# Full-height operands and dummy products in the early stage of an mLSTM and two-layer expert kernel

## The chip, the core and the metric

The kernel runs on one core of a Trainium2 chip. The metric is the device time of one execution in microseconds (us); lower is better. TensorE (PE in the rows) does matrix products, VectorE (DVE), ScalarE (ACT) and GpSimd (POOL) do elementwise work, and SyncE (SP) issues most DMA transfers.

## What is computed

Three stages follow one another: an mLSTM attention over 4 batches, 8 heads, 768 tokens and 40 dimensions; a dense layer pair with a squared ReLU; and a routed layer pair with 8 experts, one for each token. The part that the change touches is the first:

```python
for t in range(S):
    kt, vt, qt = (k[:, :, t], v[:, :, t], q[:, :, t])
    m_new = np.maximum(f_gate[:, :, t] + m, i_gate[:, :, t])
    f_stab = np.exp(f_gate[:, :, t] + m - m_new)
    i_stab = np.exp(i_gate[:, :, t] - m_new)
    m = m_new
    C = f_stab[:, :, None, None] * C + i_stab[:, :, None, None] * np.einsum('bhd,bhe->bhde', vt, kt)
    n = f_stab[:, :, None] * n + i_stab[:, :, None] * kt
    h_tilde = np.einsum('bhde,bhe->bhd', C, qt)
    nq = np.einsum('bhd,bhd->bh', n, qt)[:, :, None]
    denom = np.maximum(np.abs(nq), 1.0)
    o = 1.0 / (1.0 + np.exp(-o_gate[:, :, t]))
    y[:, :, t] = o * h_tilde / denom
# dense: relu(x @ w_in)**2 @ w_out;  routed: the same shape with the expert of the largest logit
```

## The kernel before

The recurrence is worked in 24 chunks of 128 tokens (four batches, six chunks each). Chunks 0 to 2 are the first chunks of three batches; they need no carried state. For each chunk the kernel makes, head by head, the scores of keys against queries (`scores`, tile sp, L776), multiplies them by a decay matrix (`weigh`, DVE, L781), multiplies by the values (`values`, tile pv, L789), makes the state update (`update`, tile tp, L716), divides, gates, turns the result by three transposes (`across`, tile xpt, L725), and splits it into a high and a low half for the dense layer (`columns_out`). Three chunks make one group of 384 tokens; the first layer product of a group (`l1`, tile hp, L867) can start when its three chunks are split.

The decay matrix of chunks 0 to 2 is made on TensorE by `decays_early` (tile Ap): two mask products (L659, bf16, 128 rows), then for each of two tiles four products that spread a head's decays over the columns (L663) and one that adds the bias (L665). Their operands are the running decays A, the bias c, and columns of an identity; A and c have one row for each of 36 gate rows, so these products have 36 rows. The scores of chunks 0 to 6 take keys and queries as they were loaded, in float32 with 40 rows, one for each dimension; from chunk 7 on (`WHOLE`) they take 120 rows of split operands. Odd ones among the first seven chunks load keys and queries into a tile kqs, even ones into two tiles st. `gate_stage` makes A and c on DVE and POOL from the gates; `columns` in it turns three of its rows into columns by narrow transposes (tile pt, L470).

Beside this the dense weights are decoded in 16 blocks: loaded on SP (L525), rescaled, masked and joined on ACT, POOL and DVE (L536, L544, L558, L567), rounded to a high half w_h on ACT (L570), and the rest written as a low half w_l by POOL or DVE (L583).

The order of all this up to the first layer group is written out by hand in a string, `PLAN`. Each word issues one step: `de1` the decays of chunk 1, `sc1` its scores, `va1` and `vb1` its two halves of values, `up1` its update, `tu1` its three transposes, `L3` the low half of weight block 3, `l0` the first layer product. A word `f15` issues 15 dummy products: a 128x128 tile of ones times 512 columns of ones, in bf16, into a PSUM tile that nothing reads (L1400). Ahead of the plan stand `APART` one-column products of the same kind (L1420). Each engine works its own instructions in the order in which the words issued them, and waits where an input or a buffer isn't ready.

Of the kernel before, what the change touches and what calls it, by code (L numbers as in the profile page):

```python
# [9 lines left out]
F32 = mybir.dt.float32  # L10
# [15 lines left out]
L = 128  # L26
# [27 lines left out]
XC_DVE = 2  # L54
FETCH = 2
PERIOD = 6
APART = 54

AT_ONCE = 3
WHOLE = 7  # L60
KVO = 3
QK0, QK1, ROUND0, ROUND1 = 1, 3, (3, 4), (1, 2)
PLAN = """
    g0 A0 R0 g1 qk0 kv0 g2 g3 g4 g5 g6 f15 de0 ea0 A1 g7 A2 sc0 eb0 TP0 g8 R1 vw0 g9 de1 kv1 g10 g11 S0 th0 W0 H0 R2 A3 g12 TP1 ea1 wa0 va0 L0 wb0 vb0
    S1 TP2 W1 S2 up0 qk1 eb1 qk2 di0 W2 de2 A4 R3 T3 um0 ga0 A5 sc1 H1 du0 tu0 ea2 H2 kv2 vw1 L1 eb2 g13 S3 wa1 up1 va1 L2 wb1 um1 ou0 vb1 R4 th1 sc2
    W3 TP4 di1 R5 SA4 TP5 th2 wa2 wb2 de3 qk3 ga1 f3 va2 H3 A6 vw2 up2 vb2 ca3 W4 dup1 di2 f2 tu1 cb3 de4 ga2 dup2 g14 um2 ou1 f4 tu2 sc3 ea3 ou2 S5
    H4 L3 eb3 l0 R6 L4 l1 W5 A7 wa3 kv3 l2 ca4 T6 A8 in3 wb3 H5 sa0 l3 sa1 S6 sb0 m0 va3 W6 cb4 sa2 R7 l4 sbP1 L5 T7 qk4 sb2 m1 H6 vw3 sd3 vb3 S7 sa3
    R8 sb3 T8 W7 dt A9 l5 S8 up3 sa4 H7 m2 L6 l6 di3 th3 kv4 R9 m3 sc4 sa5 um3 sbP4 L7 W8 ccP3 ea4 A10 ga3 T9 de5 dup3 m4 sa6 H8 A11 sb5 S9 wa4 vw4
    LV8 R10 ca5 th4 T10 qk5 in4 W9 up4 eb4 tu3 A12 kv5 m5 sd4 wb4 R11 l7 ea5 S10 ou3 H9 cb5 sbP6 va4 W10 um4 vb4 T11 l8 m6 eb5 sc5 sa7 A13 sb7 sa8 di4
    L9 l9 S11 W11 R12 ccP4 sbP8 qk6 T12 H10 wa5 wb5 ga4 S12 sa9 th5 vw5 H11 m7 in5 R13 T13 va5 de6 up5 A14 vb5 L10 m8 W12 sd5 sbP9 l10 LV11 m9 du4  # L70
    SA13 H12 R14 di5 l11 sc6 A15 cb6 ca6 um5 sa10 L12 sbP10 T14 tu4 l12 sa11 R15 W13 S14 H13 m10 eb6 ccP5 sb11 L13 W14 m11 ea6 wb6 kv6 H14 T15 in6 wa6
    ga5 ou4 l13 qk7 L14 sa12 th6 va6 dup5 tu5 S15 l14 sbP12 sa13 W15 sd6 sb13 vb6 de7 vw6 ra7 ou5 m12 up6 H15 m13 LV15 sa14 ca7 cb7 di6 l15 rb7 sb14
    l16 ga6 sa15 l17 m14 kv7 du6 sa16 ea7 z tu6 sb15 sb16 eb7 um6 sa17 sb17 cc6 ou6 m15
""".split()


# [298 lines left out]
def kernel(ctx, tc, qk, q3, kvo, gates, w_io, wg, w12, cst, out, dbg=None):  # L375
# [68 lines left out]
    def gate_stage():  # L444

        R = S - L
        early, late = slice(0, L), slice(L, S)
        fi = scr[0:HR, 0:2 * S]
        nc.sync.dma_start(out=fi[:, 0:2 * L], in_=gates[:, 0:2 * L])
        f, i = (fi[:, 0:L], fi[:, 2 * L:2 * L + R]), (fi[:, L:2 * L], fi[:, 2 * L + R:])  # L450

        neg, one = [scr[:, 2 * S + 64 * k:2 * S + 64 * k + 64].bitcast(BF16) for k in range(2)]
        m, a, A, c, msk = flat[0:HR, 0:S + 1], *[flat[0:HR, S * k + 1:S * k + S + 1] for k in range(1, 5)]
        wv, eA = msk, a
        yield
        nc.vector.memset(m[:, 0:1], -1e30)
        nc.gpsimd.memset(msk, 1.0)
        nc.gpsimd.memset(msk.rearrange("p (c l) -> p c l", l=L)[:, :, 0:1], 0.0)
        nc.gpsimd.memset(neg, 0.0)
        nc.gpsimd.affine_select(out=neg, in_=neg, pattern=[[1, L]], compare_op=ALU.is_ge, fill=-1e30, base=0, channel_multiplier=-1)  # L460
        nc.gpsimd.tensor_copy(out=one, in_=ident)
        early_rows.extend((neg, one, A, c))
        yield
        nc.sync.dma_start(out=fi[:, 2 * L:], in_=gates[:, 2 * L:])
        yield

        def columns(src, dst, c0, c1):
            pt = psa.tile([128, 512], F32, tag="a", name="pt")
            for ch in range(c0, c1):
                nc.tensor.transpose(out=pt[:, HR * ch:HR * ch + HR], in_=src[:, L * ch:L * ch + L], identity=ident[0:HR, 0:HR])  # L470
            nc.scalar.activation(out=dst[:, c0:c1], in_=pt[:, HR * c0:HR * c1].rearrange("p (c h) -> p c h", h=HR), func=ACTF.Copy)

        for k, (part, c0, c1) in enumerate(((early, 0, 1), (late, 1, NCH))):
            lo, hi = part.start, part.stop
            n = c1 - c0
            chunked = lambda x: x[:, part].rearrange("p (c l) -> p c l", l=L)
            nc.vector.tensor_tensor_scan(out=m[:, lo + 1:hi + 1], data0=f[k], data1=i[k], initial=m[:, lo:lo + 1] if k else -1e30, op0=ALU.add, op1=ALU.max)
            yield
            nc.vector.tensor_tensor(out=a[:, part], in0=f[k], in1=m[:, lo:hi], op=ALU.add)
            nc.gpsimd.tensor_tensor(out=c[:, part], in0=i[k], in1=m[:, lo + 1:hi + 1], op=ALU.subtract)  # L480
            yield
            nc.vector.tensor_tensor(out=a[:, part], in0=a[:, part], in1=m[:, lo + 1:hi + 1], op=ALU.subtract)
            if k == 0:
                nc.vector.memset(a[:, 0:1], 0.0)
            yield
            nc.vector.tensor_tensor_scan(out=A[:, part], data0=msk[:, part], data1=a[:, part], initial=0.0, op0=ALU.mult, op1=ALU.add)
            nc.sync.dma_start(out=A_d[:, part], in_=A[:, part])
            yield
            nc.vector.tensor_tensor(out=c[:, part], in0=c[:, part], in1=A[:, part], op=ALU.subtract)
            if k:  # L490
                columns(c, cT, 0, NCH)
            yield
            nc.vector.tensor_tensor(out=chunked(wv), in0=chunked(c), in1=chunked(A)[:, :, L - 1:L].to_broadcast([HR, n, L]), op=ALU.add)
            nc.scalar.activation(out=wv[:, part], in_=wv[:, part], func=ACTF.Exp)
            columns(wv, wT, c0, c1)
            yield
        nc.scalar.activation(out=eA[:, late], in_=A[:, late], func=ACTF.Exp)
        columns(eA, eAT, 1, NCH)
        eAL = const.tile([HR, NCH], F32, name="eAL")
        nc.vector.memset(eAL[:, 0:1], 0.0)  # L500
        nc.vector.tensor_copy(out=eAL[:, 1:NCH].rearrange("p (c o) -> p c o", o=1), in_=chunked(eA)[:, :, L - 1:L])
        nc.gpsimd.dma_start(out=L_d, in_=eAL)
        w_l.append(wts.tile([128, NF - NE, IO], F32R, tag="late", name="w_l2"))
        yield
# [98 lines left out]
    where = [divmod(n, 3) for n in range(NC)]  # L603
    first = [sum(GROUPS[:g]) for g in range(len(GROUPS) + 1)]
    xT = {}

    class Chunk:

# [13 lines left out]

        def qk(self):

            self.st = []
            odd = at1.tile([120, 2, H * L], F32, tag="kq", name="kqs") if self.n < WHOLE and self.n % 2 else None
            for j in range(2):
                st = at2.tile([120, H * L], F32, tag="st", name="st") if odd is None else odd[:, j]
                rows = D if self.n < WHOLE else 3 * D
                nc.sync.dma_start(out=st[0:rows], in_=qk[self.b, self.c, j, 0:rows])  # L630
                self.st.append(st)
            if self.c > 0:
                self.q3 = at2.tile([120, 3, L], F32, tag="q3", name="q3")
                nc.sync.dma_start(out=self.q3.rearrange("p g l -> p (g l)"), in_=q3[self.b, self.c])
# [19 lines left out]
        def decays_early(self):  # L654
            neg, one, A, c = early_rows
            self.Ab, self.Ap = [None] * 2, []
            for j in range(2):
                self.Ap.append(psa.tile([128, 4, L], F32, tag="a", name="Ap"))
                nc.tensor.matmul(self.Ap[j], one, neg.rearrange("p (o l) -> p o l", o=1).to_broadcast([128, 4, L]), start=True, stop=False)  # L659
            for j in range(2):  # L660
                for h in range(4):
                    r = HB * self.b + 2 * h + j
                    nc.tensor.matmul(self.Ap[j][:, h], ident[0:HR, r:r + 1].to_broadcast([HR, L]), A[:, 0:L], start=False, stop=False)  # L663
                r = HB * self.b + j
                nc.tensor.matmul(self.Ap[j], c[:, 0:L], ident[0:HR, r:r + 7:2].rearrange("p (h o) -> p h o", o=1).to_broadcast([HR, 4, L]), start=False, stop=True)  # L665

        def causal(self, j):
            if self.n < AT_ONCE:
# [68 lines left out]
    class Main:  # L737
# [816 lines left out]
```

## Time and profile before

| | |
|---|---|
| median of 3 runs | 796.86 us (795.98 to 800.27) |
| profiled execution, its own time | 799.19 us |
| its span, first to last instruction | 797.4 us |
| granted TensorE clock, mean over the span | 0.955 of full |
| TensorE busy | 769.4 us, 96% |
| VectorE busy | 503.2 us, 63% |
| ScalarE busy | 407.7 us, 51% |
| GpSimd busy | 388.8 us, 49% |

Read the clock beside the busy time: a busy engine at half clock passes half the columns. The ends of matmuls are modelled, so the distance from one group's start to the next tells more than the length of a row. The view of stretches gives, for each, its length, the busy time and count of each engine, and then the granted clock, the share of DMA engines and GB/s. The chain of waits is the work that ended last, followed back; each of its rows has a start, a length and the work. A timeline row has start, length, engine, line, operation, output and inputs, shapes, count, and in brackets the idle time ahead and what ended it.

### The profile page before, as it was taken

The page shows a single profiled execution, that of the slowest core. Times are in us where ns is not written, and L with a number is a line of the kernel's source. Part 1 is how long each engine was busy: PE and PEld are TensorE (multiplying, and loading weights), DVE is VectorE, ACT ScalarE, POOL GpSimd, SP SyncE. Part 2 cuts the span into 40 slices and gives each one's busy share as a digit, 9 for nine tenths or more (in the row PEclk, how much of TensorE's full clock was granted, in tenths as well). Part 3 has the DMA queues.
Part 4 walks back from the last instruction along what each step waited for, and adds up shares of the span by engine and source line. Part 5 has one row for each costly group of instructions (what it writes and reads, how often), then busy time and mean ns, then how long its engine had stood idle before and what let it go on. Part 6 is the DMA issues. An engine that isn't in the chain of part 4 may idle for free.

```text
span 797.4 us, 14304 instructions
## 1 busy us (share of the span) xinstructions
PE 769.4 (96%) x5198; PEld 744.6 (93%) x5198; DVE 503.2 (63%) x1102; ACT 407.7 (51%) x760; POOL 388.8 (49%) x430
## 2 busy tenths in 40 slices
PE   9999998989899999999999999999989999999995
PEld 6789988989899999999999999999989999999995
DVE  6448998587576676666568655362547455867553
ACT  3337776445644644644544443554246555866453
POOL 6338999455655553563445300422136444556630
PEclk8558999999999999999999999999989999999998
DMA  7367865454754445344445000100168655875620
GB/s 259 90 166 207 242 172 145 118 146 114 216 164 143 115 115 142 105 112 143 113 113 171 1 1 31 32 31 1 60 224 272 187 174 169 250 236 189 223 60 15
DMA packets 55045, 109.01 MB, mean 137 GB/s; under 512 B 6896, under 2 KB 34681, under 8 KB 54834
## 3 DMA queue, kind: packets, MB, share of 16 engines
q1 hardware_dynamic: 50370, 95.88, 40.8%
q0 software_dynamic: 4160, 11.77, 4.5%
q8 instruction: 47, 0.77, 0.4%
q10 hardware_dynamic: 432, 0.29, 0.1%
q14 instruction: 36, 0.29, 0.1%
HBM read 98.69 MB, written 10.86 MB: 137 GB/s over the span
## 4 chain that ended last, share of the span: by engine, by line
PE 73%; POOL 10%; DVE 6%; DMA 5%; issue 3%; ACT 2%; SPq 0%; POOLq 0%; DVEq 0%; ACTq 0%
PE hp L867 17%; PE hp L289 12%; PE acc L900 5%; PE acc L901 5%; PE acc L902 5%; PE pv L789 4%; DMA st<-in_qk_dram 4%; PE op L309 4%; PE op L308 4%; PE op L310 4%; POOL kq L644 3%; PE sp L776 3%; PE tp L716 2%; POOL Ab L672 2%; PE lp L965 1%
## 5 line engine op out<-in xcount | busy, mean ns | idle before, releaser
L644 POOL TENSOR_TENSOR kq<-st,kq 120x256 fp32r<-120x256 f32 x136 | 101.3, 778 | 72.8 <-ACT kq L641 72.8
L900 PE MATMUL acc<-w_h,gh 128*128 128x320 f32 x384 | 124.5, 324 | 0.0
L867 PE MATMUL hp<-xh,w_h 128*128 128x384 f32 x384 | 114.7, 353 | 5.9 <-DVE gl L887 4.2
L902 PE MATMUL acc<-w_h,gl 128*128 128x320 f32 x384 | 118.8, 310 | 1.4 <-POOL gl L887 1.4
L901 PE MATMUL acc<-w_l,gh 128*128 128x320 f32 x384 | 118.4, 308 | 0.0
L875 ACT ACTIVATE g<-hp 128x384 f32<-128x384 f32 x128 | 62.1, 485 | 89.7 <-PE hp L867 88.9
L884 DVE SCALAR_TENSOR_TENSOR hp<-hp,g 128x384 f32<-128x384 f32 x121 | 67.5, 558 | 51.1 <-ACT g L875 51.0
L258 DVE SCALAR_TENSOR_TENSOR gl<-hp,gh 128x384 fp32r<-128x384 f32 x88 | 47.0, 553 | 70.1 <-ACT gh L228 65.6
L867 PE MATMUL hp<-xh,w_l 128*128 128x384 f32 x384 | 88.7, 339 | 0.1
L867 PE MATMUL hp<-xl,w_h 128*128 128x384 f32 x256 | 87.6, 342 | 0.0
L887 DVE TENSOR_TENSOR gl<-hp,gh 128x384 fp32r<-128x384 f32 x121 | 67.5, 558 | 12.6
L902 PEld LDWEIGHTS acc<-w_h,gl 128*128 128x128 f32 x384 | 72.2, 188 | 1.7 <-POOL gl L887 1.7
L867 PEld LDWEIGHTS hp<-xh,w_h 128*128 128x128 f32 x384 | 66.2, 191 | 7.8 <-DVE gl L887 5.0
L900 PEld LDWEIGHTS acc<-w_h,gh 128*128 128x128 f32 x384 | 72.6, 189 | 0.1
L901 PEld LDWEIGHTS acc<-w_l,gh 128*128 128x128 f32 x384 | 72.6, 189 | 0.0
L876 ACT ACTIVATE gh<-g 128x384 fp32r<-128x384 f32 x128 | 67.2, 525 | 6.3 <-PE acc L901 2.3
L867 PEld LDWEIGHTS hp<-xh,w_l 128*128 128x128 f32 x384 | 69.7, 190 | 0.7 <-POOL w_l L583 0.7
L228 ACT ACTIVATE gh<-hp 128x384 fp32r<-128x384 f32 x88 | 42.7, 491 | 43.4 <-PE hp L289 36.8
L685 POOL TENSOR_TENSOR vw<-kvo,wT 128x378 f32<-128x378 f32 x20 | 18.5, 925 | 88.3 <-DMA kvo<-in_kvo_dram 46.1
L641 ACT ACTIVATE kq<-st,cs 120x1024 fp32r<-120x1024 f32 x34 | 38.9, 1145 | 41.6 <-DMA st<-in_qk_dram 38.4
L679 ACT ACTIVATE Ab<-Ab 128x512 f32<-128x512 f32 x42 | 26.2, 628 | 61.2 <-POOL Ab L673 61.0
L789 PEld LDWEIGHTS pv<-kvo,Ab 128*128 128x128 f32 x384 | 53.2, 209 | 0.6 <-issue 0.3
(277 smaller groups left out, 1925.6 us busy)
## 6 DMA issues: line engine op xcount, KB each, us to landing
st<-in_qk_dram SPq DMA_DIRECT2D x34, 480.0 KB
raw<-in_w_dram SPq DMA_DIRECT2D x30, 512.0 KB
kvo<-in_kvo_dram SPq DMA_DIRECT2D x24, 529.0 KB
raw<-in_w_io_dram SPq DMA_DIRECT2D x16, 704.0 KB
Ab<-A_d SPq DMA_DIRECT2D x42, 256.0 KB
raw<-in_w_dram SPq DMA_DIRECT2D x20, 427.0 KB
raw<-in_w_dram SPq DMA_DIRECT2D x10, 426.0 KB
q<-in_q_dram SPq DMA_DIRECT2D x20, 180.0 KB
```

The source lines that it names most:

```text
L258: e.scalar_tensor_tensor(out=gl[:, j], in0=hp[j % 4], scalar=0.0, in1=gh[:, j].bitcast(F32), op0=ALU.max, op1=ALU.subtract).then_inc(sGL, 1)
L289: m = e.matmul(hp[f % 4][:, 0:w], a, c, start=(n == 0), stop=(n == 7))
L644: nc.gpsimd.tensor_tensor(out=o[:, c], in0=self.st[j][:, c], in1=o[:, c].bitcast(F32), op=ALU.subtract)
L789: nc.tensor.matmul(self.pv[:, hd], d.Ab[r][:, i], d.v[:, hd], start=True, stop=True)
L867: nc.tensor.matmul(hp, a, x, start=(n == 0), stop=(n == 7))
L875: nc.scalar.activation(out=r, in_=hp, func=ACTF.Relu)
L876: nc.scalar.activation(out=gh, in_=r, func=ACTF.Square)
L884: e.scalar_tensor_tensor(out=sq, in0=hp, scalar=0.0, in1=r, op0=ALU.max, op1=ALU.mult)
L887: e.tensor_tensor(out=gl, in0=sq, in1=gh.bitcast(F32), op=ALU.subtract)
L900: nc.tensor.matmul(acc[t][:, 0:DM], gh[:, sl], wh, start=(f == 0), stop=False)
L901: nc.tensor.matmul(acc[t][:, 0:DM], gh[:, sl], wl, start=False, stop=False)
L902: nc.tensor.matmul(acc[t][:, 0:DM], gl[:, sl], wh, start=False, stop=end)
```

## The change

It has three parts. The products of `decays_early` take all 128 rows of A, c and the identity, and the scores of chunks 0 to 6 take 120 rows of keys and queries; the rows that held nothing are set to zero once, by memsets on DVE, in tiles that live through the early chunks. A word `f2`, two dummy products, stands in `PLAN` ahead of nearly each early product group, 22 times, in place of `f3`, `f2` and `f4`. `APART` goes from 54 to 19.

```diff
-APART = 54
+APART = 19
-    S1 TP2 W1 S2 up0 qk1 eb1 qk2 di0 W2 de2 A4 R3 T3 um0 ga0 A5 sc1 H1 du0 tu0 ea2 H2 kv2 vw1 L1 eb2 g13 S3 wa1 up1 va1 L2 wb1 um1 ou0 vb1 R4 th1 sc2
+    L0 wb0 f2 vb0 S1 TP2 W1 S2 f2 up0 qk1 eb1 qk2 di0 W2 f2 de2 A4 R3 T3 um0 ga0 A5 f2 sc1 H1 du0 f2 tu0 ea2 H2 kv2 vw1 L1 eb2 f2 g13 S3 wa1 f2 up1 f2 va1
...
+        A0, cc0 = [flat[:, S * k + 1:S * k + 1 + L] for k in (2, 3)]
         yield
+        for x in padded[0]:
+            nc.vector.memset(x, 0.0)
+        nc.vector.memset(A0, 0.0)
+        nc.vector.memset(cc0, 0.0)
...
-        early_rows.extend((neg, one, A, c))
+        early_rows.extend((neg, one, A0, cc0))
...
+            if k == 0:
+                nc.vector.memset(kqs, 0.0)
             columns(wv, wT, c0, c1)
...
+    kqs = at1.tile([120, 2, H * L], F32, tag="kq", name="kqs")
+    padded = [[at2.tile([120, H * L], F32, tag="st", name="st") for _ in range(2)], [kqs[:, 0], kqs[:, 1]]]
...
+            self.st = padded[self.n % 2] if self.n < WHOLE else [at2.tile([120, H * L], F32, tag="st", name="st") for _ in range(2)]
+            rows = D if self.n < WHOLE else 3 * D
             for j in range(2):
+                nc.sync.dma_start(out=self.st[j][0:rows], in_=qk[self.b, self.c, j, 0:rows])
...
-                    nc.tensor.matmul(self.Ap[j][:, h], ident[0:HR, r:r + 1].to_broadcast([HR, L]), A[:, 0:L], start=False, stop=False)
+                    nc.tensor.matmul(self.Ap[j][:, h], ident[:, r:r + 1].to_broadcast([128, L]), A, start=False, stop=False)
-                nc.tensor.matmul(self.Ap[j], c[:, 0:L], ident[0:HR, r:r + 7:2].rearrange("p (h o) -> p h o", o=1).to_broadcast([HR, 4, L]), start=False, stop=True)
+                nc.tensor.matmul(self.Ap[j], c, ident[:, r:r + 7:2].rearrange("p (h o) -> p h o", o=1).to_broadcast([128, 4, L]), start=False, stop=True)
...
-                k, q = (d.st[j][0:D, c] for j in range(2)) if n < WHOLE else (d.kq[:, j, c] for j in range(2))
+                k, q = (d.st[j][:, c] for j in range(2)) if n < WHOLE else (d.kq[:, j, c] for j in range(2))
```

TensorE, from the narrow transposes of c (pt) through the values of chunk 0 (pv) and its update (tp) to the masks of the third decays (Ap), before:

```order
L470 MATMUL pt<-cs,flat 128x36 x6
L789 MATMUL pv<-kvo,Ab 128x42 x8
L716 MATMUL tp<-vw,kvo 120x126 x3
L659 LDWEIGHTS scr
L659 MATMUL Ap<-scr 128x512
```

The same place in the changed kernel, where the lines of the file have moved by six:

```order
L475 MATMUL pt<-cs,flat 128x36 x6
L1406 LDWEIGHTS ones
L1406 MATMUL warm<-ones 128x512
L1406 LDWEIGHTS ones
L1406 MATMUL warm<-ones 128x512
L795 MATMUL pv<-kvo,Ab 128x42 x4
L1406 LDWEIGHTS ones
L1406 MATMUL warm<-ones 128x512
L1406 LDWEIGHTS ones
L1406 MATMUL warm<-ones 128x512
L795 MATMUL pv<-kvo,Ab 128x42 x4
```

A pair of dummies now stands between the transposes and the values and between the two halves of values; the order of the other work is the same.

DVE, from the start of the program to the first operation on the late gates (640 columns), before:

```order
L456 MEMSET flat 36x1
L477 SCALAR_TENSOR_TENSOR flat<-scr 36x128
L479 TENSOR_TENSOR flat<-scr,flat 36x128
L482 TENSOR_TENSOR flat<-flat 36x128
L484 MEMSET flat 36x1
L486 SCALAR_TENSOR_TENSOR flat<-flat 36x128
L489 TENSOR_TENSOR flat<-flat 36x128
L493 TENSOR_TENSOR flat<-flat 36x128
L477 SCALAR_TENSOR_TENSOR flat<-scr,flat 36x640
```

And the first rows of the changed kernel, in two pieces:

```order
L458 MEMSET st 120x1024 x2
L459 MEMSET flat 128x128
L460 MEMSET flat 128x128
L461 MEMSET flat 36x1
L482 SCALAR_TENSOR_TENSOR flat<-scr 36x128
```

```order
L498 TENSOR_TENSOR flat<-flat 36x128
L501 MEMSET kqs 120x2048
L482 SCALAR_TENSOR_TENSOR flat<-scr,flat 36x640
```

The memsets of st and of the rows of A and c stand ahead of the first scan, that of kqs behind the early gate work and ahead of the late scan. On SP the loads into st now wait for their memset.

## Rows read from the trace of the kernel before

**Rows 1.** Stretches: busy time and count by engine, granted clock, DMA.

```profile
core 0: us, PE busy (x) PEld busy (x) DVE busy (x) ACT busy (x) POOL busy (x), PEclk, DMA share, GB/s
5.00:10.00 5.00, 5.00 (x24) 2.58 (x23) 2.49 (x4) 0.84 (x1) 1.32 (x2) 1.00 0.96 262
10.00:15.00 5.00, 5.00 (x30) 3.72 (x28) 4.90 (x5) 2.63 (x6) 2.86 (x2) 0.78 0.88 357
15.00:20.00 5.00, 5.00 (x17) 3.64 (x17) 3.76 (x5) 1.53 (x2) 4.75 (x4) 0.50 0.66 207
65.00:70.00 5.00, 5.00 (x26) 5.00 (x25) 4.49 (x7) 2.98 (x6) 3.51 (x4) 0.76 0.71 209
70.00:75.00 5.00, 5.00 (x37) 5.00 (x36) 4.00 (x6) 4.94 (x9) 4.92 (x5) 1.00 0.63 67
170.00:180.00 10.00, 7.54 (x45) 7.10 (x45) 7.12 (x29) 3.45 (x9) 1.04 (x2) 0.83 0.85 243
```

**Rows 2.** The chain of waits, 0 to 150 us: start, length, work.

```profile
1.01 1.61 PE apart L1420 x54
2.66 5.00 PE warm L1400 x15
7.66 0.43 PE Ap L659 x2
...
11.79 0.03 PE pt L470
...
55.42 0.85 PE warm L1400 x2
56.28 0.64 PE xpt L725 x3
56.92 0.68 PE pt L470 x5
...
63.77 6.05 PE hp L867 x24
...
73.19 0.82 PE pv L789 x8
74.01 1.46 PE hp L867 x8
...
79.07 0.65 PE tp L716 x6
...
84.62 0.82 POOL vw L685
...
135.66 0.35 SPq L630
```

**Rows 3.** Timeline of TensorE: spread decays (36 rows) and scores (40 rows).

```profile
8.02 1.15 PE L663 MATMUL Ap<-flat,cs 36*128 36x128 f32 x8
...
83.67 2.05 PE L776 MATMUL sp<-st 40*128 40x128 f32 x16
```

**Rows 4.** Timeline of DVE: the gate work and one weight step.

```profile
3.10 0.42 DVE L477 TENSOR_TENSOR_SCAN flat<-scr 36x128 f32<-36x128 f32 x1 [2.22 <-DMA scr<-in_gates_dram]
...
5.71 0.28 DVE L493 TENSOR_TENSOR flat<-flat 36x128 f32<-36x128 f32 x1
8.05 1.55 DVE L477 TENSOR_TENSOR_SCAN flat<-scr,flat 36x640 f32<-36x640 f32 x1 [2.05 <-DMA scr<-in_gates_dram]
...
12.74 0.86 DVE L558 SCALAR_TENSOR_TENSOR raw<-raw 128x704 int32<-128x704 int32 x1
```

**Rows 5.** Timeline of POOL: low halves of weights and two squares, with waits.

```profile
58.73 1.70 POOL L583 TENSOR_TENSOR w_l<-raw,w_h 128x704 fp32r<-128x704 f32 x1
61.34 1.69 POOL L583 TENSOR_TENSOR w_l<-raw,w_h 128x704 fp32r<-128x704 f32 x1 [0.91 <-ACT w_h L570]
...
69.59 0.83 POOL L886 TENSOR_TENSOR g<-g 128x384 f32<-128x384 f32 x1 [1.41 <-ACT gh L876]
...
77.34 1.20 POOL L886 TENSOR_TENSOR g<-g 128x384 f32<-128x384 f32 x1 [1.03 <-ACT gh L876]
```

More of the change, by code (lines that the diff above doesn't have):

```diff
@@ L63 @@
 PLAN = """
-    g0 A0 R0 g1 qk0 kv0 g2 g3 g4 g5 g6 f15 de0 ea0 A1 g7 A2 sc0 eb0 TP0 g8 R1 vw0 g9 de1 kv1 g10 g11 S0 th0 W0 H0 R2 A3 g12 TP1 ea1 wa0 va0 L0 wb0 vb0
-    S1 TP2 W1 S2 up0 qk1 eb1 qk2 di0 W2 de2 A4 R3 T3 um0 ga0 A5 sc1 H1 du0 tu0 ea2 H2 kv2 vw1 L1 eb2 g13 S3 wa1 up1 va1 L2 wb1 um1 ou0 vb1 R4 th1 sc2
-    W3 TP4 di1 R5 SA4 TP5 th2 wa2 wb2 de3 qk3 ga1 f3 va2 H3 A6 vw2 up2 vb2 ca3 W4 dup1 di2 f2 tu1 cb3 de4 ga2 dup2 g14 um2 ou1 f4 tu2 sc3 ea3 ou2 S5
-    H4 L3 eb3 l0 R6 L4 l1 W5 A7 wa3 kv3 l2 ca4 T6 A8 in3 wb3 H5 sa0 l3 sa1 S6 sb0 m0 va3 W6 cb4 sa2 R7 l4 sbP1 L5 T7 qk4 sb2 m1 H6 vw3 sd3 vb3 S7 sa3
@@ L68 @@
[L68 to L71, printed above, removed]
@@ L72 @@
-    ga5 ou4 l13 qk7 L14 sa12 th6 va6 dup5 tu5 S15 l14 sbP12 sa13 W15 sd6 sb13 vb6 de7 vw6 ra7 ou5 m12 up6 H15 m13 LV15 sa14 ca7 cb7 di6 l15 rb7 sb14
-    l16 ga6 sa15 l17 m14 kv7 du6 sa16 ea7 z tu6 sb15 sb16 eb7 um6 sa17 sb17 cc6 ou6 m15
+    g0 A0 R0 g1 qk0 kv0 g2 g3 g4 g5 g6 f15 de0 ea0 A1 f2 g7 A2 f2 sc0 eb0 TP0 g8 R1 vw0 g9 f2 de1 kv1 g10 g11 S0 th0 W0 H0 R2 A3 f2 g12 TP1 ea1 wa0 f2 va0
+    L0 wb0 f2 vb0 S1 TP2 W1 S2 f2 up0 qk1 eb1 qk2 di0 W2 f2 de2 A4 R3 T3 um0 ga0 A5 f2 sc1 H1 du0 f2 tu0 ea2 H2 kv2 vw1 L1 eb2 f2 g13 S3 wa1 f2 up1 f2 va1
@@ new lines @@
+    L2 wb1 um1 ou0 f2 vb1 R4 th1 f2 sc2 W3 TP4 di1 R5 SA4 TP5 th2 wa2 wb2 de3 qk3 ga1 f2 va2 H3 A6 vw2 f2 up2 f2 vb2 ca3 W4 dup1 di2 f2 tu1 cb3 de4 ga2
+    dup2 f2 g14 um2 ou1 f2 tu2 f2 sc3 ea3 ou2 S5 H4 L3 eb3 l0 R6 L4 l1 W5 A7 wa3 kv3 l2 ca4 T6 A8 in3 wb3 H5 sa0 l3 sa1 S6 sb0 m0 va3 W6 cb4 sa2 R7 l4
+    sbP1 L5 T7 qk4 sb2 m1 H6 vw3 sd3 vb3 S7 sa3 R8 sb3 T8 W7 dt A9 l5 S8 up3 sa4 H7 m2 L6 l6 di3 th3 kv4 R9 m3 sc4 sa5 um3 sbP4 L7 W8 ccP3 ea4 A10 ga3 T9
+    de5 dup3 m4 sa6 H8 A11 sb5 S9 wa4 vw4 LV8 R10 ca5 th4 T10 qk5 in4 W9 up4 eb4 tu3 A12 kv5 m5 sd4 wb4 R11 l7 ea5 S10 ou3 H9 cb5 sbP6 va4 W10 um4 vb4 T11
@@ new lines @@
+    l8 m6 eb5 sc5 sa7 A13 sb7 sa8 di4 L9 l9 S11 W11 R12 ccP4 sbP8 qk6 T12 H10 wa5 wb5 ga4 S12 sa9 th5 vw5 H11 m7 in5 R13 T13 va5 de6 up5 A14 vb5 L10 m8
+    W12 sd5 sbP9 l10 LV11 m9 du4 SA13 H12 R14 di5 l11 sc6 A15 cb6 ca6 um5 sa10 L12 sbP10 T14 tu4 l12 sa11 R15 W13 S14 H13 m10 eb6 ccP5 sb11 L13 W14 m11
+    ea6 wb6 kv6 H14 T15 in6 wa6 ga5 ou4 l13 qk7 L14 sa12 th6 va6 dup5 tu5 S15 l14 sbP12 sa13 W15 sd6 sb13 vb6 de7 vw6 ra7 ou5 m12 up6 H15 m13 LV15 sa14
+    ca7 cb7 di6 l15 rb7 sb14 l16 ga6 sa15 l17 m14 kv7 du6 sa16 ea7 z tu6 sb15 sb16 eb7 um6 sa17 sb17 cc6 ou6 m15
@@ L623, in qk @@
         def qk(self):
-            self.st = []
-            odd = at1.tile([120, 2, H * L], F32, tag="kq", name="kqs") if self.n < WHOLE and self.n % 2 else None
+            self.st = padded[self.n % 2] if self.n < WHOLE else [at2.tile([120, H * L], F32, tag="st", name="st") for _ in range(2)]
+            rows = D if self.n < WHOLE else 3 * D
             for j in range(2):
[L628 to L631, printed above, removed]
+                nc.sync.dma_start(out=self.st[j][0:rows], in_=qk[self.b, self.c, j, 0:rows])
             if self.c > 0:
```

## The prediction, made before the result was known

> **What bounds the kernel now.** I read the granted clock by stretch first, then the chain of waits, then the timelines of the engines that could be late next. In the stretches [rows 1] the reader is to see two things. [...] The clock is full from 5 us, falls inside 10 to 15 us and comes back inside 65 to 70 us. TensorE was not idle before it fell: it went from the 15 dummy products of 128 rows to products whose operands have 36 rows, which stand at 8.02 us and after [rows 3], and then to scores of 40 rows. It came back after the first 128-row layer products at 63.77 us [rows 2]. The fall inside 170 to 180 us is of another kind, since TensorE was busy for 7.54 of 10 us there [rows 1].
>
> The chain of waits lies on TensorE without a break from 1.01 us to the first layer product at 63.77 us and beyond; POOL takes it over only near 84.62 us and keeps it to 135.66 us [rows 2]. So at half clock the early stage is TensorE's own work, and every microsecond saved there is real until another engine is late.
>
> **The cause as I read it.** A stream of few-row operands counts as little activity, although the engine never waits. [...]
>
> **The change part by part.**
>
> TensorE, from the first decays product to the first layer product. Before it took 63.77 - 7.66 = 56.1 us [rows 2]. At full clock I take each group from a row at 1.00:
> - three groups of decays: the first one ran at full clock, 11.79 - 7.66 = 4.13 us [rows 2]; 3 x 4.13 = 12.4. No row shows one product at both heights. The nearest are the updates, of 128 rows, 0.65 us for three of 126 columns [rows 2], 0.22 each, and the scores, of 40 rows, 2.05 us for eight of 128 columns [rows 3], 0.26 each: the taller ones are not dearer, so the padding itself costs nothing on TensorE.
> - four groups of scores at 2.05 us, the row of a 40-row group at full clock [rows 3]: 8.2.
> - six half groups of values at 0.82 us [rows 2]: 4.9.
> - three updates at 0.65 us [rows 2]: 2.0.
> - nine transposes of a chunk, three of which took 0.64 us at half clock: 3 x 0.32 = 1.0. Seventeen narrow transposes, five of which took 0.68 us at half clock [rows 2]: 17 x 0.068 = 1.2. (Half the price at twice the clock is an estimate for both.)
> - 22 pairs of dummies. A pair of 512 columns took 0.43 us at full clock (the two masks at 7.66 us) and 0.85 us at half (the pair at 55.42 us) [rows 2]: 22 x 0.43 = 9.5. The nine dummies that stood there go; they are in the 56.1.
>
> The sum is 39.2 us. I add 0.4, about one dummy pair, for short waits that half clock hides now: behind the scores of the third chunk only one pair stands ahead of the values, which want DVE's weighting of those scores. That makes 39.6 us, 16.5 less than before. The start gains a little: 35 of the 54 one-column products go, which took 1.61 us for all [rows 2], so 1.0 us; part of it is lost again if the clock rises at the same moment and more of the 15 dummies run at half clock. I take 0.7. The first decays product then stands at 7.0 us and the first layer product at 46.6 us, 17.2 us earlier. The first three layer groups, 6.05 us at mostly half clock, take 3 x 1.46 = 4.4 us at full [rows 2]: 1.7 more, so TensorE is 18.9 us ahead there.
>
> The memsets. No DVE memset of this size is in the trace. The nearest row is a DVE operation on 704 elements in 0.86 us [rows 4], 1.2 ns an element; the two of 1024 and the two of 128 elements cost at most 2.8 us by that, and nothing at the least. I take half to all of it. DVE is free until the gates land at 3.10 us, so the scan starts by 3.7 us at the latest, and its result, ready at 5.99 us before [rows 4], by 6.6 us: TensorE wants it behind 7.4 us. Hidden. Without that cover it would be 0.6 us. Two things queue behind: the first loads of keys and queries on SP wait for the memset, and the value load and the write of the decays stand behind them on SP, at most 1 us late; the scores want the keys near 12 us. The 2048-element memset (at most 2.5 us) lies after 5.99 us, and DVE's next input comes at 8.05 us [rows 4], so at most 1.1 us spills into the late scan, which its user, the narrow transposes near 18.5 us, does not see. The padded tiles are the same buffers as before, so no load waits longer for a free one.
>
> What is late next. Behind the last values product (its end is the dummies' start at 55.42 us) come ScalarE, DVE and POOL steps that don't know TensorE's clock, up to the low-half subtraction at 58.73 us [rows 2, 5]: 3.3 us. In the changed order that product ends 46.6 minus what TensorE still has to do: four dummy pairs 1.7, six chunk transposes 0.6, five narrow ones 0.3, scores 2.05, and the 0.4 of waits, so at 41.6 us. POOL starts this block at 44.9 us, 13.8 us earlier. From there POOL is nearly dense up to 135.66 us, and carries the chain from 84.62 us on [rows 2]. It has three waits in it that go back to TensorE or the decode ahead of it: 0.91, 1.41 and 1.03 us [rows 5], 3.4 in all. TensorE being 18.9 us ahead, most of them close. So the gain that comes out of the POOL stage lies between 13.8 and 17.2 us. I take 16.5, near the upper end, since the two longer waits are for ScalarE results of layer products, which move by more than POOL. Behind 135.66 us TensorE bounds again and everything shifts by that.
>
> **The forecast.** The profiled execution took 799.2 us, 2.3 more than the median of 796.9; the gain applies to either: 782.7 by that execution, 780.4 by the median. I give 780.4.
>
> **Rivals.**
> 1. *The clock isn't held.* If zero rows count for nothing, or rows are not what the gate weighs, TensorE falls to 0.50 soon after 12 us as now, and the dummies are pure load. TensorE's 56.1 us lose nine dummies (3.8) and gain 44 at half clock (22 x 0.85 = 18.7): 71.0 us, 14.9 more, less 0.7 to 1 at the start. All of it stands ahead of the chain: 796.9 + 14 = 811. It decides by when the clock is lost: lost for good before some 25 us the dummies outweigh the part run fast; after that there is still a gain. For it: no row shows a product with zero rows. Against it: dummies with ones alone lift the share of full-row columns ahead of every group, and the start shows that they count. [...] Chance 0.12.
> 2. *The clock is lost for a while*, in decays or scores between the dummies, and comes back with the next dense group. Each lost 10 us of stretch costs some 5: a gain of 4 to 12, 785 to 793. Chance 0.13.
> 3. *The other engines don't follow.* With 16 us less to cover them, the decode steps of DVE, ScalarE and POOL and the weight loads crowd, and a step that now has its input early has it late. Then TensorE runs at full speed but waits: a gain of 8 to 13, 784 to 789. Waits could also drop the clock. Chance 0.13.
> 4. The forecast: clock held to the first layer products, gain 13.8 to 18.5. Chance 0.62.
>
> A small scatter lies on all: the later fall inside 170 to 180 us [rows 1] happens where TensorE waits, and whether the chip catches such a wait may change with the shift; that is worth 1 to 3 us either way.
>
> **Numbers.** The range takes in the forecast with that scatter and rivals 2 and 3: 776 to 793. The slower case stays out with 0.12. A difference under 0.5% (4 us) can't be told from none in a measurement like this. Faster by more: 0.62 + 0.13 + nearly all of rival 2, 0.85; within: 0.04; slower: 0.11.
>
> **What would show it.** Right: granted clock 1.00 in all of 10 to 50 us; decays groups of 4.1 us instead of 8; the first layer product near 46 to 47 us; POOL's subtraction of the fourth weight block near 45 us; dummies at 0.43 us a pair. Wrong: a clock of 0.50 in the second or third decays group (rival 1 or 2), or idle TensorE with DVE or POOL as releaser between 20 and 46 us (rival 3). If the first layer product is 17 us earlier but the end of the POOL stage only 10, the third rival has it.

## The result and the profile after

The changed kernel took 784.85 us (median of four executions, 783.44 to 786.91), the kernel before beside it 796.98 (795.98 to 800.27): a ratio of 0.9843, 95% interval 0.9803 to 0.9882. The profiled execution took 783.44 us, with a span of 781.6.

The stretches of the changed kernel, with the columns of [rows 1]:

```profile
5.00:10.00 5.00, 5.00 (x29) 3.31 (x28) 4.09 (x5) 1.65 (x3) 1.41 (x3) 1.00 0.96 279
10.00:15.00 5.00, 5.00 (x33) 3.42 (x32) 4.86 (x6) 1.93 (x4) 3.17 (x2) 1.00 0.83 336
15.00:20.00 5.00, 5.00 (x34) 3.34 (x32) 4.97 (x5) 2.37 (x5) 4.66 (x4) 1.00 0.45 136
20.00:30.00 10.00, 10.00 (x71) 7.90 (x71) 8.75 (x14) 5.39 (x10) 7.20 (x5) 1.00 0.72 219
30.00:40.00 10.00, 9.87 (x77) 7.99 (x74) 6.17 (x12) 5.32 (x9) 3.57 (x5) 1.00 0.62 176
40.00:50.00 10.00, 9.87 (x67) 8.25 (x66) 8.88 (x14) 5.18 (x10) 9.68 (x11) 1.00 0.91 253
```

The clock stays at 1.00 through the whole early stage from its rise at 5.5 us on. In 15 to 20 us TensorE is as busy as before, 5.00 of 5 us, and passes 34 records at 1.00 where it passed 17 at 0.50 [rows 1].

The chain of waits of the changed kernel, the pieces that answer to [rows 2]:

```profile
1.01 0.68 PE apart L1426 x19
1.73 5.23 PE warm L1406 x15
6.97 0.43 PE Ap L665 x2
...
12.05 1.79 PE sp L782 x16
...
56.37 1.46 PE hp L873 x8
...
68.75 0.82 POOL vw L691
```

The decays start 0.69 us earlier than before (6.97 for 7.66), POOL's weighting of the values (vw) 15.9 us earlier (68.75 for 84.62). The timelines of TensorE, POOL and DVE around the first layer products show what lies between:

```profile
45.93 0.60 PE L873 MATMUL hp<-xh,w_h 128*128 128x384 f32 x2
...
51.49 0.93 PE L722 MATMUL tp<-C,q 120*128 120x126 f32 x6 [1.12 <-DVE Ab L787]
```

```profile
44.34 3.38 POOL L590 TENSOR_TENSOR w_l<-raw,w_h 128x704 fp32r<-128x704 f32 x2
...
53.49 0.83 POOL L892 TENSOR_TENSOR g<-g 128x384 f32<-128x384 f32 x1 [1.17 <-ACT gh L882]
```

```profile
7.04 1.76 DVE L501 MEMSET kqs<- 120x2048 f32 x1 [0.37 <-issue]
8.73 1.42 DVE L482 TENSOR_TENSOR_SCAN flat<-scr,flat 36x640 f32<-36x640 f32 x1
...
45.28 4.19 DVE L565 SCALAR_TENSOR_TENSOR raw<-raw 128x704 int32<-128x704 int32 x1
...
50.74 1.29 DVE L787 TENSOR_TENSOR Ab<-sp,Ab 128x512 f32<-128x512 f32 x2
```

The first layer product stands at 45.93 us (63.77 in the chain of before), the fourth low half on POOL at 44.34 (58.73 in [rows 5]). Here the lead of TensorE meets the other engines: behind the three layer groups TensorE waits 1.12 us for the weighted scores, which stand on DVE behind a weight step (L565) of 4.19 us; the same step of before took 2.40 us:

```profile
61.38 2.40 DVE L558 SCALAR_TENSOR_TENSOR raw<-raw 128x704 int32<-128x704 int32 x1
```

POOL worked two low halves in a row just then (3.38 us), before one at a time (1.69). The step is about as long (4.35 us) in two kernels further down where POOL does the same, the dummies alone and the change with short decays. That POOL makes it longer was not tested, and the change's step at 27.22 us took 0.88 us beside a low half of 2.81 us that POOL had begun at 26.82.

In these two profiles nothing more is won or lost from there on. The three products of tile lpt, some 70 us later, come at 123.9 us (139.5 before), 15.6 earlier, and the profiled execution ends 15.75 us earlier (783.44 for 799.19).

### The profile page after: what moved, and what is told of

Read it like the earlier page. It is cut to its first block, busy times and chain, and to the rows that moved or that the text cites. A ratio compares the mean times of both kernels' runs of the same rounds, so it can differ in the third digit from the quotient of the medians.

```text
span 781.6 us, 14309 instructions
## 1 busy us (share of the span) xinstructions
PE 752.0 (96%) x5198; PEld 728.5 (93%) x5198; DVE 512.5 (66%) x1107; ACT 407.8 (52%) x760; POOL 392.5 (50%) x430
## 4 chain that ended last, share of the span: by engine, by line
PE 70%; DVE 10%; POOL 8%; DMA 5%; issue 4%; ACT 3%; SPq 0%; DVEq 0%; POOLq 0%; ACTq 0%
PE hp L873 16%; PE hp L289 11%; PE acc L906 5%; PE acc L908 5%; PE acc L907 5%; DMA st<-in_qk_dram 4%; PE op L309 4%; PE op L308 4%; PE op L310 4%; PE pv L795 3%; POOL kq L650 3%; PE sp L782 2%; PE warm L1406 2%; PE tp L722 2%; POOL Ab L678 2%
## 5 line engine op out<-in xcount | busy, mean ns | idle before, releaser
L647 ACT ACTIVATE kq<-st,cs 120x1024 fp32r<-120x1024 f32 x34 | 38.9, 1145 | 44.7 <-DMA st<-in_qk_dram 39.8
L685 ACT ACTIVATE Ab<-Ab 128x512 f32<-128x512 f32 x42 | 26.2, 627 | 58.7 <-POOL Ab L679 58.4
L171 POOL DMA_INDIRECT out_dram<-ot,idx x34 | 39.9, 1173 | 28.1 <-ACT ot L207 20.6
```

## The experiments

Each was timed beside the kernel before. "First layer product" is the start of the first product of tile hp, "lpt" that of the first of tile lpt; the changed kernel has 45.9 and 123.9, the kernel before 63.7 and 139.5.

### The dummies alone

The kernel before with the new `PLAN` and the new `APART`; operands stay at 36 and 40 rows.

```diff
-APART = 54
+APART = 19
-    ... A1 g7 A2 sc0 eb0 ... g9 de1 ... W2 de2 ... A5 sc1 ...
+    ... A1 f2 g7 A2 f2 sc0 eb0 ... g9 f2 de1 ... W2 f2 de2 ... A5 f2 sc1 ...
```

> The 22 pairs of dummies and the shorter start alone; operands stay at 36 and 40 rows, no memsets. Theory A (the height of the operands carries the clock): the clock falls to 0.50 in the first or second decays group and stays there until the layer products; the dummies cost 0.85 us a pair, the first layer product stands near 70 to 78 us, the time is 803 to 812 us. Theory B (dummies ahead of each group are enough): clock 1.00 from 6 us on, first layer product near 46 us, time 783 to 787 us as with the whole change.

Measured: 795.73 us (793.95 to 800.94), ratio 0.9984, interval 0.9959 to 1.0009; first layer product 63.6, lpt 141.4. Its stretches:

```profile
10.00:20.00 10.00, 10.00 (x36) 6.49 (x35) 8.66 (x9) 3.44 (x6) 8.02 (x5) 0.58 0.79 287
20.00:30.00 10.00, 10.00 (x34) 5.89 (x32) 1.76 (x2) 1.33 (x3) 0.22 (x1) 0.50 0.33 94
30.00:40.00 10.00, 10.00 (x43) 6.14 (x41) 5.71 (x9) 4.20 (x8) 3.66 (x3) 0.67 0.21 72
40.00:50.00 10.00, 10.00 (x44) 7.55 (x43) 1.89 (x4) 2.40 (x5) 2.07 (x3) 0.55 0.18 56
50.00:60.00 10.00, 9.98 (x75) 7.66 (x74) 7.00 (x14) 4.48 (x8) 5.11 (x6) 1.00 0.78 216
```

The clock falls as before, to 0.50 in 20 to 30 us, so dummies between short operands don't hold it. But it rises for a while in 30 to 40 us and is full from about 49, where before had 0.50 until past 65 [rows 1]. What that gives back is about what the dummies cost: no change that can be measured.

### The padding alone

The changed kernel with the `PLAN` and the `APART` of before, so with its nine dummies. It ran twice, with other kernels beside it.

```diff
-APART = 19
+APART = 54
-    ... A1 f2 g7 A2 f2 sc0 eb0 ... g9 f2 de1 ... ga1 f2 va2 ...
+    ... A1 g7 A2 sc0 eb0 ... g9 de1 ... ga1 f3 va2 ...
```

> The padding with its memsets alone; the plan and its nine dummies and the 54 one-column products as before. Theory A: clock 1.00 through the decays; the early stage of TensorE is shorter than with the dummies by some 13 pairs more (44 less 9 at 0.216 us, 7.6 us), less what the other engines then hold up; first layer product at 39 to 44 us, time 778 to 785 us. Theory B: the clock falls near 13 us as before, time 795 to 800 us. In between: it falls in the values and updates, which have few columns, and comes back in the next decays; 785 to 793 us.

> The padding with the order of before and its nine dummies, a second time with more rounds, beside the others on one chip. Theory (the padding alone makes the change's gain, and the 22 pairs add nothing that can be measured): 781 to 786, within 0.4% of the change's 785. Rival (its 782.7 was a lucky draw and the dummies do buy something by the clock that they hold): 786 to 789, as without any dummies.

Measured: 782.72 us (779.77 to 786.45), ratio 0.9824, interval 0.9772 to 0.9875; again 783.63 (780.22 to 787.11), ratio 0.9829, interval 0.9799 to 0.9859. The first profile loses the clock for some 7 us, the second not at all before 97 us:

```profile
30.00:40.00 10.00, 9.32 (x53) 8.58 (x53) 6.92 (x14) 5.92 (x10) 4.72 (x5) 0.66 0.64 176
```

```profile
30.00:40.00 10.00, 8.94 (x74) 7.59 (x73) 7.99 (x16) 6.08 (x12) 4.96 (x7) 1.00 0.75 209
```

First layer products stand at 46.6 and 43.0, lpt at 125.1 and 121.4. So the padding carries the gain, with or without the 22 pairs. With the clock held, the first layer product stands 2.9 us earlier than the change's (43.0 for 45.9); with the clock lost for 7 us it stands 0.7 later. So the pairs cost about what such a fall costs. The two profiles of the change differ by 0.4 us there, those of the padding by 3.6; two of each are too few to call the early stage with pairs the steadier one.

### The change a second time

> The changed kernel once more, for the spread between executions. If its two times (783.5 and 786.5) come from the falls of the clock later in the program, the profile shows another set of falls than the first one's (162.5, 196.6 and 568.7 us) and the same first layer product near 46 us; the time is 783 to 787 us. If the early stage varies, the first layer product moves by 1 us or more between the two profiles.

Measured: 784.98 us (782.13 to 786.83), ratio 0.9857, interval 0.982 to 0.9895; in the profile the clock is full from 6.4 to 566 us, first layer product 46.3, lpt 124.4. The early stage came out the same, 39.0 us from the first decays product to the first layer product (39.1 in the first profile); the executions differ by where the decays start and by what happens later.

### Which operands matter

First, the change with decays and bias products of 36 rows again:

```diff
-matmul(self.Ap[j][:, h], ident[:, r:r + 1].to_broadcast([128, L]), A, ...)
+matmul(self.Ap[j][:, h], ident[0:HR, r:r + 1].to_broadcast([HR, L]), A[0:HR], ...)
-matmul(self.Ap[j], c, ident[:, r:r + 7:2]...to_broadcast([128, 4, L]), ...)
+matmul(self.Ap[j], c[0:HR], ident[0:HR, r:r + 7:2]...to_broadcast([HR, 4, L]), ...)
```

> The change, with the decays and bias products taking 36 rows again; scores keep their 120 rows, the dummies stay. Theory (rows of the operands hold the clock, and a few tall products between short ones only bridge): a decays group is over 4 us of nothing but 36-row products, so the clock falls during or behind the first group near 11 to 12 us, as with the dummies alone (11.5), comes back with the taller scores and dummies, and is lost again by one of the next two groups. First layer product at 50 to 58 us instead of 46, time 787 to 793. Rival (the scores are what matters, since there are four groups of them and they stand amid waits): first layer product at 46 to 48, time 783 to 787. Second rival (the decays are all that matters): first layer product above 60, time 794 to 800.

Measured: 787.97 us (784.15 to 793.11, and one execution of 796.56), ratio 0.987, interval 0.9841 to 0.9898; in the profile, of the execution that took 793.11, first layer product 57.4, lpt 135.5. Its stretches:

```profile
10.00:20.00 10.00, 10.00 (x61) 6.29 (x60) 8.62 (x10) 4.06 (x8) 7.08 (x5) 1.00 0.75 280
20.00:30.00 10.00, 10.00 (x42) 7.40 (x41) 6.56 (x9) 3.65 (x7) 3.78 (x3) 0.51 0.62 183
30.00:40.00 10.00, 10.00 (x34) 7.09 (x34) 1.99 (x4) 2.49 (x4) 3.32 (x3) 0.50 0.00 1
40.00:50.00 10.00, 9.88 (x73) 7.78 (x73) 5.66 (x12) 5.31 (x9) 1.49 (x2) 0.96 0.53 144
```

The fall came at 20.2 us, behind the second decays group and not the first as I had put it, and the clock came back once, at 40.7. First layer product and median lie in the theory's ranges. But this profile stands for three of the seven executions: their mean clock is 0.979 and they took 792.2 to 796.6 us. The other four have 0.989 to 0.993, like the change, and took 784.2 to 788.0. A stretch of 20 us at half clock takes 0.013 off the mean, so these four did not lose it that long: with tall scores and the dummies the clock was held even between short decays, in some executions. All memsets are still in this kernel, so they are not what holds it.

Then the change with scores of 40 rows again:

```diff
-k, q = (d.st[j][:, c] for j in range(2)) if n < WHOLE else ...
+k, q = (d.st[j][0:D, c] for j in range(2)) if n < WHOLE else ...
```

> The change, with the scores of the first seven chunks taking 40 rows again; the decays and bias products keep 128 rows, the dummies stay. Theory: a group of scores is 2 us long and has dummies ahead of it, so the clock is held through most of it and falls once at most, near 30 to 45 us: first layer product at 46 to 50 us, time 784 to 789. Rival (scores matter as much as decays): two falls or more before 45 us, first layer product above 52, time 789 to 795.

Measured: 783.52 us (781.76 to 785.59), ratio 0.9822, interval 0.9795 to 0.985; one fall, first layer product 47.9, lpt 125.6:

```profile
30.00:40.00 10.00, 9.98 (x69) 7.62 (x68) 5.87 (x12) 5.31 (x9) 4.02 (x6) 0.93 0.66 165
40.00:50.00 10.00, 9.95 (x63) 7.80 (x62) 6.88 (x13) 5.09 (x10) 7.15 (x8) 0.90 0.88 249
```

The fall is where the theory had it, and the first layer product comes 2 us later; the time is no longer than the change's. So the padding of the decays is the larger part, where it shows at all: without it the clock was lost for 20 us in the profile, by the mean clock in three of seven executions, and the median is 3 us longer. That of the scores is worth less than the executions scatter.

### Half the dummies, and fewer still

One dummy for each pair, and then none of these up to the scores of the second chunk, 13 in all:

```diff
-    ... A1 f2 g7 A2 f2 sc0 eb0 ... A5 f2 sc1 H1 du0 f2 tu0 ...
+    ... A1 f1 g7 A2 f1 sc0 eb0 ... A5 f1 sc1 H1 du0 f1 tu0 ...
```

```diff
-    ... A1 f2 g7 A2 f2 sc0 eb0 ... A5 f2 sc1 H1 du0 f2 tu0 ...
+    ... A1 g7 A2 sc0 eb0 ... A5 sc1 H1 du0 f1 tu0 ...
```

> The change with one dummy in place of each pair: 22 x 0.21 = 4.7 us of TensorE less ahead of the first layer product. Theory (TensorE is ahead of POOL and VectorE by then, so its own time no longer counts): first layer product at 42 to 46 us, the fourth low half on POOL at 43 to 45 us, first low-half transposes of the layer result near 123 to 125 as in the change, time 782 to 787. Rival (TensorE's time still bounds): all of it 4 to 5 us earlier, time 779 to 782. Second rival (half the dummies don't hold the clock): a fall between 28 and 45 us as in the kernel with no dummies, time 786 to 790.

> The change with one dummy in place of each pair, and none at all up to the scores of the second chunk: 13 dummies are left. Theory (the padded stream holds the clock by itself until some 33 us, as the kernels with nine or no dummies showed, falling at 33.1 and 33.5; later single dummies bridge what follows; all TensorE time ahead of the first layer product is on the path): 9 x 0.21 = 1.9 us less than with 22 singles, so first layer product at 41 to 42 us, the fourth low half on POOL near 40, first low-half transposes near 119.5, time 779.5 to 782. Rival (VectorE and POOL bound by then): first layer product at 41 to 42, but first low-half transposes at 121 as with 22 singles, time 782 to 783. Second rival (the early dummies are part of what holds the clock later): a fall between 20 and 45 us, first layer product at 43 to 46, time 783 to 788.

Measured with 22 singles: 782.25 us (782.14 to 783.39), ratio 0.981, interval 0.9786 to 0.9833; clock 1.00 from 5.4 to 97 us, lpt 121.4. Where TensorE stands, then POOL, and its waits in 6 to 50 us (total, count, longest), of which the view lists none for the changed kernel:

```profile
43.23 0.60 PE L873 MATMUL hp<-xh,w_h 128*128 128x384 f32 x2
```

```profile
41.85 3.37 POOL L590 TENSOR_TENSOR w_l<-raw,w_h 128x704 fp32r<-128x704 f32 x2
```

```profile
PE tp L722 <- DVE Ab L787: 1.4, 1, 1.4
PE xpt L731 <- POOL kvo L847: 1.1, 2, 0.6
PE pt L475 <- ACT flat L499: 0.6, 1, 0.6
PE pv L795 <- DVE Ab L787: 0.3, 1, 0.3
```

Of 4.7 us of TensorE work taken out, 2.7 arrive at the first layer product and 2.5 at POOL and at lpt. The time fell into the range of the theory, but what happened is what the rival said, by half: TensorE's time in the early stage does count, and the rest turns into waits.

Measured with 13 singles: 782.56 us (777.89 to 785.23), ratio 0.9811, interval 0.9786 to 0.9835; no fall from 7.5 to 563.9 us, but first layer product 44.7 and lpt 122.9. Theory and first rival missed the place; the second rival had it (43 to 46), but by a fall that didn't come. The decays started 1.1 us later than with 22 singles, and TensorE waited more, among others:

```profile
26.09 1.83 PE L782 MATMUL sp<-kqs 120*128 120x128 f32 x14 [0.81 <-DVE C L818]
...
42.44 0.55 PE L731 MATMUL xpt<-cs,kvo 128*128 128x128 f32 x3 [0.87 <-POOL kvo L847]
```

There the other engines bound, and fewer dummies buy nothing more: the padding with nine dummies and its clock held had lpt at the same 121.4 as 22 singles. Both medians lie some 2 to 3 us under the change's. Intervals of the ratios (up to 0.9835) reach over those of the change (from 0.9803), so a better kernel is likely with 22 singles and not shown.

### No dummies at all, and what that does 600 us later

The change without any of the 22 pairs; it ran twice.

```diff
-    ... A1 f2 g7 A2 f2 sc0 eb0 ... dup2 f2 g14 um2 ou1 f2 tu2 f2 sc3 ...
+    ... A1 g7 A2 sc0 eb0 ... dup2 g14 um2 ou1 tu2 sc3 ...
```

> The whole change without its 22 pairs; the 15 dummies at the start stay, and the 19 one-column products. Theory A: as the padding alone, 1 us or less from it either way, 777 to 785 us, the first layer product at 38 to 43 us. If dummies hold the clock through the values and updates between the second and the third chunk: a fall to 0.50 somewhere in 20 to 45 us and 786 to 797 us.

> The padding without any of the 22 pairs, a second time. Theory (it loses the clock for some 7 us near 35 to 45, and that is all): first layer product at 43 to 47 us, first low-half transposes at 121 to 124, time 782 to 786 by this profile, later stages as in the change. Rival (what it loses lies later, in stages that the edit doesn't touch, by where the later falls land): first layer product and first low-half transposes as above, but the end 3 us or more later than they give, time 787 to 790.

Measured: 789.0 us (785.04 to 793.0), ratio 0.9901, interval 0.9871 to 0.9932; again 792.18 (786.78 to 793.39), ratio 0.9926, interval 0.9899 to 0.9953. Clearly slower than the padding with nine dummies, though its early stage isn't: the clock is lost for some 7 us in both profiles, first layer products stand at 46.7 and 44.1, lpt at 123.6 and 120.6, the last one 3.3 us ahead of the change. The rival had it: what is lost is lost later (792.18 is 2 us past its range). Two numbers on record say where. The mean clock of the 15 executions is 0.981 (0.973 to 0.989), of the change's eight 0.990 (0.983 to 0.994): 0.009 of some 785 us, so by estimate some 14 us more at half clock, worth 7 us of time at the most. And in the routed layers, from the first to the last start of a product with w0h (L289), it is 205.5 and 205.1 us, where the profiles of the other kernels above have 198.8 to 201.5. TensorE's timeline there, in the second profile:

```profile
718.72 0.59 PE L289 MATMUL hp<-xh,w0h 128*128 128x384 f32 x2 [1.95 <-issue]
...
720.18 0.34 PE L289 MATMUL hp<-xh,w0h 128*128 128x384 f32 x1
722.03 0.44 PE L289 MATMUL hp<-xh,w0h 128*128 128x384 f32 x1 [1.51 <-issue]
```

And in the first:

```profile
718.15 0.34 PE L289 MATMUL hp<-xh,w0h 128*128 128x384 f32 x1
721.87 0.45 PE L289 MATMUL hp<-xh,w0h 128*128 128x384 f32 x1 [3.38 <-issue]
```

Both stand still at the same place, after nine products of the same run of layer products, and the profile names no engine and no transfer that they wait for. The view of the transfers over the standstill of the first profile, 718.4 to 722 us, has one packet of an instruction queue beside those of the two data queues (packets, MB, share of the 16 transfer engines):

```profile
q0 software_dynamic: 115, 0.35, 25.1%
q1 hardware_dynamic: 35, 0.09, 6.2%
q8 instruction: 1, 0.02, 1.8%
```

By the trace that packet starts at 719.5 us; in the second profile one starts at 719.9, 0.7 us ahead of the standstill, and runs into it. The pages count the packets of this queue over the whole program, here and in the changed kernel:

```profile
q8 instruction: 49, 0.80, 0.4%
```

```profile
q8 instruction: 47, 0.77, 0.4%
```

My reading is that TensorE's own instructions arrived late there; the trace doesn't show when they arrive, only the packets of that queue. Before, the change and all others with as many products on TensorE (5,198, each with a weight load) have 47 packets; this kernel has 5,154 products and 49 packets in both profiles, with the instructions of the other engines unchanged. The 35 one-column products that the change takes away and the nine old dummies are as many as the 44 new ones. A shorter program alone is not enough: with 13 singles (5,167 products, 48 packets) the routed layers take 198.8 us. So I filled the program up again.

```diff
-APART = 19
+APART = 63
```

> The padding without any of the 22 pairs, but with 63 one-column products at the start in place of 19, so that TensorE's program has 5,891 instructions, as many as before (the kernel with 19 has 5,803). Both profiles with 5,803 showed waits of the kind issue ahead of the last layer products (L289), 9.8 and 10.4 us in six, where the change shows 2.3 in two. Theory (these waits hang on where the program's instructions stand, and they are what that kernel loses in stages that it doesn't touch): the issue waits at L289 go back to 2 to 3 us, first layer product at 42 to 47 us, median 780 to 784. Rival (it loses by the clock, which falls for 7 us in the early stage and then later): issue waits as in the change or not, median 787 to 792. Second rival (the waits come from transfers that run at that moment): issue waits of 5 us or more at L289 again, median 786 to 791.

Measured: 787.07 us (783.46 to 791.22) beside a kernel before that took 802.62 on that chip, so only the ratio compares: 0.9805, interval 0.9768 to 0.9843, apart from both intervals of the unfilled kernel. Its early stage was no better (half clock for 6.8 us, first layer product 47.1, lpt 124.0). The same products in its timeline now run through, though an instruction packet comes within these 6 us as well:

```profile
718.52 0.51 PE L289 MATMUL hp<-xh,w0h 128*128 128x384 f32 x2
...
719.91 0.51 PE L289 MATMUL hp<-xh,w0h 128*128 128x384 f32 x2
```

By the numbers set down beforehand the theory did not come out. The median lies in the ranges of both rivals, if on a slower chip, and the waits of the kind issue at L289 sum to 6.1 us in six, where the theory had 2 to 3 and the second rival 5 or more. That sum counts a standstill twice, once for the products and once for the weight loads: the products alone waited 2.7 us, against 4.8 and 4.5 unfilled and 1.0 in the change. From the first to the last product with w0h it is 203.0 us, some 2 less than unfilled and 2 more than the change's 200.8; a wait of 2.3 us stands at another place instead, ahead of line L275 at 604 us. The mean clock, 0.982, is hardly above the 0.981 of the unfilled kernel. So the standstill at that place went when the program was filled up, which speaks for the place of the instructions and against transfers at that moment, and the clock has its part in what is left. One profile on another chip does not show more, and how the loss divides stays open. That the late arrival of instructions makes these waits is read from the packets and the lengths of the programs, not shown directly.

### The kernel before, a second profile

> The kernel before, a second profile. Theory (its early stage is the same in each execution and its spread comes from where falls land later): first layer product at 63 to 64.5 us, the fourth low half on POOL at 58 to 59.5, first low-half transposes at 139 to 140, whatever the end. Rival (the spread arises early, by when the clock falls and rises): first layer product away from 63.7 by over 1.5 us.

Measured: 799.84 us; first layer product 63.7, fourth low half on POOL 58.7, lpt 139.5, all within 0.1 us of the first profile. The early stage of before repeats; it differs from the first profile by falls of the clock behind 176 us.

## Why the prediction was right, point by point

**The cause** was read rightly. The clock fell because the operands had few rows, not because TensorE waited: in 20 to 30 us TensorE is busy for 10.00 of 10 us at 0.50 with the dummies alone, and for 10.00 of 10 us at 1.00 in the change, the same kernel with zero rows. Padding alone holds it too, but for some 7 us in one of two profiles. What rival 1 left open, whether zero rows count, is settled for this kernel: they do.

**The early stage.** TensorE took 39.1 us from the first decays product to the first layer product (6.80 to 45.93 in the timeline), forecast 39.6. That it is so close is in part luck. The three decays groups and the four of scores took 1.7 us less than their terms: the 2.05 us of a group of scores was the length of a row [rows 3], while from one start to the next the change has 1.78 at 120 rows, and the kernel with scores of 40 rows 1.98. The pairs with the short waits took 0.9 more, the narrow transposes 0.3. Padding made neither the scores nor the decays dearer; a group of decays at full clock now has a row at both heights, before first:

```profile
9.88 1.05 PE L663 MATMUL Ap<-flat,cs 36*128 36x128 f32 x8
```

```profile
8.99 1.05 PE L669 MATMUL Ap<-flat,cs 128*128 128x128 f32 x8
```

The short waits came where I had put them, behind the scores of the third chunk, and at two more places: there a pair of dummies is 0.72, 0.61 and 0.73 us ahead of what follows, where most have 0.43, some 0.8 us in all for the 0.4. The view of waits lists none of them, since the ends of products are modelled. The first one:

```profile
36.76 0.60 PE L1406 MATMUL warm<-ones 128*128 128x512 bf16 x2
37.48 1.09 PE L795 MATMUL pv<-kvo,Ab 128*128 128x42 f32 x8
```

The start gained 0.69 of the 0.7, and that was luck: in the second profiles of both kernels the first decays product stands at 7.27 and 7.29 us, since the clock rose at 6.4 us in the change and at 5.5 in before.

**The memsets** cost 0.91 us for 1024 elements, 0.17 for 128, 1.76 for 2048: the first four 2.16 in sum, under their bound of 2.8. The late scan started 0.68 us later (8.73 for 8.05), and TensorE's view of waits shows no user of it in the change. With 22 singles the narrow transposes wait 0.6 us for the late gate work.

**The engines that follow.** POOL's fourth low half came at 44.34, forecast 44.9. Behind it POOL gained on: 14.4 us ahead there, 15.9 at vw, 15.6 at lpt. I had 16.5 out of 13.8 to 17.2. The waits of 0.91 and 1.03 us are gone, that of 1.41 is still 1.17 [rows 5], and one of 0.48 for DVE stands ahead of vw. So the third rival has its part, 0.9 us, at the place where TensorE waits 1.12 us for DVE.

**The end.** By the two profiled executions the gain is 15.75 us, 782.7 forecast and 783.44 measured. By the medians it is 12.1, the point forecast of 780.4 was 4.4 us too low, and 784.85 lies where rival 3 had it (784 to 789), not in the forecast's own gain of 13.8 to 18.5. The step that failed is the sentence that "the gain applies to either". The profiled execution of before lay 2.2 us over its median, that of after 1.4 under its own: these 3.6 us and the 0.75 that POOL kept make the difference. The second profiles, 799.84 and 782.13 us, lie to the same sides and are 17.7 apart. I carried a gain read from the rows of single executions over to medians. Falls of the clock at places that change from one execution to the next (177 to 180 us in [rows 1], none up to 566 us in the change's second profile) go with it: of 19 executions of the kernel before on one chip, the two with a mean clock of 0.965 took 794.8 and 795.0 us, the two with 0.953 took 800.3 and 801.7. Why the profiled ones lie on these sides was not settled.

**Rival 1** had the wrong price. With the clock lost, 811 us was the sum, since the dummies were pure load; the dummies alone measured a ratio of 0.9984. The step that failed is that TensorE's time would "gain 44 at half clock" and nothing else: they brought full clock back over 15 us earlier, which paid for them.

## What to carry to other kernels

Where TensorE is busy without a gap at half clock, look at how many rows its operands have: zero rows up to 120 or 128 cost nothing on TensorE here (1.05 us for eight products of the decays at 36 and at 128 rows, 1.98 and 1.78 us for a group of scores at 40 and at 120), and the stream of decays, the longest of such products, was the one whose padding mattered more. The 22 pairs bought nothing beyond the padding that could be measured here (0.9843 and 0.9857 with them, 0.9824 and 0.9829 with nine dummies), so pad first and add dummies only if they are seen to pay. After taking instructions out of a long program, look for waits without a releaser far from the edit (4.8 and 4.5 us at L289 here, 1.0 in the change) before the loss is put down to the edit itself. Look at the mean clock of every execution before one profile is taken for the kernel, and compare medians with medians.

## What the runs showed that I had not expected

- With 88 instructions less in TensorE's first 45 us, waits of 1.5 to 3.4 us stood at the same product some 670 us later in both profiles, and the queue of instructions carried 49 packets for 47. With 88 cheap ones put in at the start these were gone (ratios 0.9901 and 0.9926 against 0.9805), but not the whole loss.
- The granted clock rose between 4.4 and 7.5 us after the start in the profiles of these kernels, with much the same 15 dummies (at 5.9 in the kernel before, where the prediction has 5), and the later falls came at other places each time. The executions of one kernel spread over 1.3 us (22 singles) to 9 us (decays of 36 rows).
- With decays of 36 rows one and the same kernel lost the clock for 20 us in its profile, and by their mean clock four of its seven executions did not.
- Dummies of 128 rows amid products of 36 and 40 rows did not hold the clock but brought it back over 15 us earlier than the kernel before had it.
